# Attention scores as 64-row products in both halves of the array, V kept in float32, on one Trainium2 core

## The chip, the cores and the metric

The program runs on one core of one Trainium2 chip. The metric is the device time of one execution in microseconds; the time before is the median of three runs. A core has TensorE (PE, matrix products; its weight loads are listed as PEld), VectorE (DVE), ScalarE (ACT), GpSimd (POOL), and SyncE (SP, which here only issues DMAs). The granted clock of TensorE is given as a share of full speed: 1.00 is 2.4 GHz and 0.50 is 1.2 GHz, its two levels.

## The reference

```python
# q, k, v: (4, 8, 576, 64); M_prev (4, 8, 64, 64), z_prev (4, 8, 64), beta (8)
scores = where(causal, -1e9, (q @ k.T) / 8)
a = exp(scores - scores.max(-1)); a /= a.sum(-1) + 1e-9
local = a @ v
phi = lambda x: where(x > 0, x, exp(x) - 1) + 1
mem = (phi(q) @ M_prev) / (phi(q) @ z_prev + 1e-6)
g = 1 / (1 + exp(-beta))
x = (g * mem + (1 - g) * local)          # reshaped to 2304 rows of 512
# x is the input of a mixture of 8 experts with 1024 hidden columns, one expert for each row:
logits = normalised(x) @ normalised(expert_emb).T / tau
e = argmax(logits);  out = softmax(logits)[e] * (relu(x @ w1[e]) @ w2[e])
```

## The kernel before

Attention is done in eight groups: one of four batches and four of its eight heads. The 576 query rows of a head are cut into tiles i = 0 to 3 of 128 rows and a tail i = 4 of 64 rows, two tails of a head pair together. Causality leaves (i + 1) x 128 key columns for tile i. A score tile of 128 rows is a unit, and goes through the steps S (score products into a PSUM bank `aux`), M (VectorE adds the mask and takes the row's maximum, L725), E (ScalarE, exponential, L753), T (TensorE, transposes, L762), H and L (L772 on ScalarE and L776 on VectorE: the transposed weights as a float16 high and low part) or P (one float32 copy, L786), and C (products with V into a bank `L`).

Each group is prepared by `prep_group`: q and k are transposed on TensorE (L601), split into a high part (fp32r) and a low part, and phi(q) is formed on POOL (L667, L668: `qp`). Query and key operands are stacked by nine DMAs a group from SBUF to SBUF, so that the high parts of a head's keys stand twice, on rows 0 to 63 and 64 to 127, and the query's high and low part one above the other. A score tile is then two products for each head: one over 128 rows (L712, high and low queries with high keys) and one over 64 rows (L713, high queries with low keys). Only tiles 0 and 1 of group 0 are made directly of 64-row products (L708 to L710), since they go ahead of the first stacking.

V is prepared by `prep_v`: absolute maximum over each partition (L543, VectorE), over the partitions (`partition_all_reduce`, L547, POOL), a power of two from it (VectorE), and V scaled and split into float16 high (`vh`, L569, POOL) and low (`vl`, L572, VectorE). In tiles 0 and 3 a block of weights and V are three float16 products (L808 to L810); tiles 1, 2 and the tails use one float32 product of 65 columns (L800, L818): 64 of V and a column of ones, which gives the row's sum.

The memory term phi(q) M comes from L899; L918 to L949 put both terms together into rows X, on VectorE and POOL; `route_ops` (L983 to L1048) normalises them and forms the logits. `batch_ops` ranks rows by expert, and writes row numbers to a table in DRAM (`id_dram`) by scatters on POOL (L1128), each waiting for the one before. Three early slots of 128 rows of the first expert run ahead of the main loop of slots (L1516 layer 1, L1586 layer 2); their weights are split into high and low on ScalarE, VectorE and POOL (L1316, L1328).

The order of instructions on every engine up to the main loop is made in advance by a list scheduler (`Sched`): estimated durations (`c_act`, `c_dve` and numbers written at each `op`), priorities (`PRIO`), and rings of buffers (six PSUM banks `aux`, two `L`). Where it expects TensorE to wait near the start it inserts products that nobody reads (L255). Every engine keeps its order, so an instruction that waits holds all behind it on that engine.

Of the kernel before, what the change touches and what calls it, by code (L numbers as in the profile page):

```python
# [34 lines left out]
# Priorities and choices of the list scheduler.  # L35
PRIO = {'po': {'S': 0.5860956202798256, 'M': -2.5, 'E': 0.17467982721190245, 'T': 0.2779440791838692, 'H': -1.149000400638553, 'L': -1.05503872663039, 'C': -0.2719843589915537}, 'pa': 0.4405403455875509, 'pv': 10.001535500524492, 'sq': 2.536521872945253, 'xt': 2, 'ra': 2, 'aD': 1, 'ps': 0.775235707503454, 'lv': 2.568625074006147, 'pr': 5.21426841392578, 'rs': 1, 'w1p': 203.44655206520034, 'ag': 0, 'pb': 7.884706576128789, 'lqk': 8.346887064301836, 'rr': 0, 'aA': 1, 'pe4': 1, 'ep': 108.76714709039749, 'w2p': 229.1293559788917, 'slack': 65.79007591242566, 'pp': 1.1250262799121031, 'fc': (1, 2), 'nw2l': 2, 'nw1l': 2, 'xlo': 1, 'wpd': 2, 'w1': 300000, 'ND': 2, 'avl': 2, 'ph': 1, 'avc': 1, 'phat': 10154.340622343301, 'ae': 1}


class Sched:
    """Static list scheduler: orders single-engine steps by estimated start time, with bounded buffer rings."""  # L40
# [19 lines left out]
    def run(self, slack=80.0):  # L60
# [106 lines left out]
def kernel(  # L167
# [23 lines left out]
    ASC = 16384.0  # L191
# [32 lines left out]
    id_dram = dr.tile([PADN, 2], I32, name="id_dram")  # L224
# [4 lines left out]
    RB = cst.tile([P, 8704], F32R, name="RB")  # L229
# [5 lines left out]
    er_t = [[RA[:, 5120 + S * (2 * s + c) : 5120 + S * (2 * s + c) + S] for c in range(2)] for s in range(2)]  # L235
    loq_t = RB[:, 0:1280].rearrange("p (x n) -> p x n", x=2)
    hi_t = RB[:, 1280:3840].rearrange("p (x c n) -> p x c n", x=2, c=2)
    kh_t = [RB[:, 3840:6400].rearrange("p (x j n) -> p x j n", x=2, j=2), wk.tile([P, 2, 2, 640], F32R, tag="kh1", name="kh1")]
    lok_t = [t.rearrange("p (x n) -> p x n", x=2) for t in (RB[:, 6400:7552], RC[:, 5632:6784])]
    kl1_t = [t.rearrange("p (x n) -> p x n", x=2) for t in (RB[0:64, 7552:8704], RC[0:64, 6784:7936])]  # L240
    qs_t = [RC[:, 2816 * i : 2816 * i + 2816].rearrange("p (x j n) -> p x j n", x=2, j=2) for i in range(2)]
    qp_t = [wk.tile([P, 2, S], F32, tag=f"qp{i}", name=f"qp{i}") for i in range(2)]
    qd_t = [cst.tile([P, 2, P], F32R, name=f"qd{i}") for i in range(2)]
    VN = [wk.tile([P, NFULL + 1, 4, 65], F32, tag=f"VN{i}", name=f"VN{i}") for i in range(3)]
    VHt = [wk.tile([P, NFULL, 4, 65], F16, tag=f"vh{i}", name=f"vh{i}") for i in range(2)]
    VLt = [wk.tile([P, NFULL, 4, D], F16, tag=f"vl{i}", name=f"vl{i}") for i in range(2)]
# [19 lines left out]
    ND = cfg.get("ND", 2)  # L266

    # A unit is a 128-row score tile: the query rows of index i of some heads of one group.
    units, UB = [], []
    for gi, (b, g) in enumerate(groups):  # L270
        UB.append(float(len(units)))
        pairs = ((0, 2), (1, 3)) if gi == 0 else ((0, 1), (2, 3))
        if gi == 0 and ND > 0:
            units += [dict(gi=gi, i=0, hs=list(p)) for p in pairs]
        else:
            units.append(dict(gi=gi, i=0, hs=[0, 1, 2, 3]))
        if gi == 0 and ND < 2:
            pairs = ((0, 1), (2, 3))
        units += [dict(gi=gi, i=1, hs=list(p)) for p in pairs]
        units += [dict(gi=gi, i=i, hs=[h]) for i in (2, 3) for h in range(4)]  # L280
        units += [dict(gi=gi, i=4, x=x, hs=[2 * x, 2 * x + 1]) for x in range(2)]
    for n, u in enumerate(units):
        u["n"] = n
        u["b"], u["g"] = groups[u["gi"]]
        u["blocks"] = [(hh, kb) for hh in u["hs"] for kb in range(u["i"] + 1)] if u["i"] < 4 else range(4)
        u["direct"] = u["gi"] == 0 and u["i"] < ND
# [4 lines left out]
    # -------------------------------------------------------------- constants  # L291
    for t in qs_t:
        nc.gpsimd.memset(t[:, :, :, 0:64].bitcast(F32), 0.0)
    for t in qd_t:
        nc.gpsimd.memset(t.bitcast(F32), 0.0)
    nc.gpsimd.memset(hi_t[:, :, :, 64:128].bitcast(F32), 0.0)
    nc.gpsimd.memset(loq_t[:, :, 64:128].bitcast(F32), 0.0)
# [8 lines left out]
    for j in range(2):  # L306
# [4 lines left out]
        )  # L311
    for t in VN:
        nc.gpsimd.memset(t[:, :, :, D : D + 1], 1.0)
    for t in VHt:
        nc.gpsimd.memset(t[:, :, :, D : D + 1], 1.0)
# [36 lines left out]
    def c_pad_dma():  # L352
        nc.sync.dma_start(id_dram.rearrange("(p n) c -> p n c", p=P), padt)
# [44 lines left out]
    # -------------------------------------------------------- the experts' unit vectors  # L398
# [4 lines left out]
    def newton_steps(dst, src, s_, r_):  # L403
        """Steps of dst = sqrt(src): exponent-halving start, Newton iterations; tiny src is lifted off zero."""
# [15 lines left out]
    def chain(tag, steps, deps, prio, eng="DVE", dur=75):  # L420
# [15 lines left out]
    def en_load():  # L436
# [12 lines left out]
            # 1 / tau = tm * te with 1 <= |tm| < 2  # L449
# [27 lines left out]
    # ------------------------------------------------------------------ loads  # L477

    def load_qk(b):
        for g in range(2):  # L480
            gi, hs = 2 * b + g, slice(4 * g, 4 * g + 4)
            for s in (1, 0):
                for n in (NFULL, *range(NFULL)):
# [7 lines left out]
                    deps = () if b == 0 else tuple(("pe", gi - 2, x, s if n < NFULL else 2) for x in range(2))  # L491
# [34 lines left out]
    # ------------------------------------------------------- operand preparation  # L526
    VS = {}

    def prep_v(gi):
        b, g = groups[gi]  # L530
        st = {}
        pr = (0.0 if gi == 0 else ub(gi - 1) + cfg.get("pv", 6.0))
        lv = tuple(("lv", gi, n) for n in range(NFULL))
        vn = lambda: VN[SL["VN", gi]]
        mx, ma, scl, scw = (cst.tile([P, w], F32, name=f"v{nm}{gi % 2}") if gi < 2 else None
                            for nm, w in (("mx", 1), ("ma", 1), ("sc", 1), ("sw", 4)))
        if gi < 2:
            VS[gi] = (mx, ma, scl, scw)
        mx, ma, scl, scw = VS[gi % 2]
        dv = tuple(("d2", gi - 2, i) for i in range(5)) if gi >= 2 else ()  # L540

        def amax():
# [283 lines left out]
    def unit_ops(u):  # L826
# [6 lines left out]
        if 1 in js:  # L833
            sh += (("sh", gi, "kl", 1),)
# [1008 lines left out]
```

## Time and profile before

| | |
|---|---|
| time, median of three runs | 728.16 us (728.54, 725.67, 728.16) |
| span of the profiled execution | 719.1 us, by its trace; no time of its own beside it |
| PE, DVE, ACT, POOL busy, share of the span | 88%, 55%, 44%, 37% |
| attention, to the first early layer-1 product | 395.0 us |
| early slots, to the first main layer-1 product | 58.3 us |
| main loop of slots | 251.7 us |
| last output transfers | 14.1 us |

The median stands 9.1 us above the span: that much lies around it. The first three stages overlap a little (weights are split while attention ends), so the borders are those of TensorE's order: L1516 first runs at 395.0 us and, for the main loop, at 453.3 us.

### The profile page before, as it was taken

The page shows a single profiled execution, that of the slowest core. Times are in us where ns is not written, and L with a number is a line of the kernel's source. Part 1 is how long each engine was busy: PE and PEld are TensorE (multiplying, and loading weights), DVE is VectorE, ACT ScalarE, POOL GpSimd, SP SyncE. Part 2 cuts the span into 40 slices and gives each one's busy share as a digit, 9 for nine tenths or more (in the row PEclk, how much of TensorE's full clock was granted, in tenths as well). Part 3 has the DMA queues.
Part 4 walks back from the last instruction along what each step waited for, and adds up shares of the span by engine and source line. Part 5 has one row for each costly group of instructions (what it writes and reads, how often), then busy time and mean ns, then how long its engine had stood idle before and what let it go on. Part 6 is the DMA issues. An engine that isn't in the chain of part 4 may idle for free. (4 is left out here: it accounts for less than half of the span.)

```text
span 719.1 us, 12737 instructions
## 1 busy us (share of the span) xinstructions
PE 635.5 (88%) x3798; PEld 498.2 (69%) x3798; DVE 398.4 (55%) x1182; ACT 316.0 (44%) x646; POOL 267.9 (37%) x338
## 2 busy tenths in 40 slices
PE   7298969999998999969998876999999989988872
PEld 6267657877786787858786755777877767766651
DVE  5245535774555363734577852158535874686460
ACT  5136435764554553645467411144224541463340
POOL 6213622643735425726258343211322222231120
PEclk9658776997587585995799996999999998999996
DMA  6948860694734934405567109147734687488530
GB/s 133 213 107 185 193 145 7 156 212 84 174 87 105 203 78 105 112 7 130 99 229 161 46 6 308 40 71 195 203 91 105 207 262 201 102 228 237 161 80 13
DMA packets 153622, 98.49 MB, mean 137 GB/s; under 512 B 129080, under 2 KB 129208, under 8 KB 153538
## 3 DMA queue, kind: packets, MB, share of 16 engines
q1 hardware_dynamic: 148738, 87.02, 50.7%
q0 software_dynamic: 4800, 10.52, 4.8%
q8 instruction: 32, 0.52, 0.3%
q14 instruction: 52, 0.43, 0.2%
HBM read 110.69 MB, written 10.67 MB: 169 GB/s over the span
## 5 line engine op out<-in xcount | busy, mean ns | idle before, releaser
L1586 PE MATMUL L<-RC,hhl 128*128 128x512 f32 x528 | 140.0, 423 | 25.9 <-ACT hhl L1560 15.8
L1586 PEld LDWEIGHTS L<-RC,hhl 128*128 128x128 f32 x528 | 105.3, 203 | 53.6 <-ACT hhl L1560 17.1
L1516 PE MATMUL aux<-RB,xhl 128*128 128x512 f32 x528 | 129.8, 398 | 2.0 <-ACTq L1462 1.0
L1516 PEld LDWEIGHTS aux<-RB,xhl 128*128 128x128 f32 x528 | 98.5, 189 | 26.8 <-ACTq L1462 1.4
L725 DVE CUSTOM_DVE_ANT_0 a<-aux,mask 128x128 f32<-128x128 f32 (+3 forms) x144 | 62.6, 455 | 66.8 <-PE aux L713 59.4
L1447 POOL DMA_INDIRECT a<-x_dram,ix x22 | 23.8, 1081 | 149.6 <-DMA ix<-id_dram 111.8
L762 PE MATMUL aux<-ident,a 128*128 128x128 f32 x384 | 75.2, 333 | 3.8 <-ACT a L753 2.5
L753 ACT ACTIVATE a<-a,nb 128x128 f32<-128x128 f32 (+3 forms) x128 | 66.6, 556 | 15.2 <-DVE nb L725 10.3
L800 PE MATMUL L<-VN,aT 128*128 128x65 f32 x320 | 61.0, 351 | 6.7 <-ACT aT L786 6.4
L800 PEld LDWEIGHTS L<-VN,aT 128*128 128x128 f32 x320 | 57.3, 267 | 11.9 <-ACT aT L786 7.5
L762 PEld LDWEIGHTS aux<-ident,a 128*128 128x128 f32 x384 | 54.2, 174 | 13.4 <-ACT a L753 4.8
L786 ACT ACTIVATE aT<-aux 128x512 f32<-128x512 f32 (+1 forms) x80 | 37.0, 486 | 47.5 <-PE aux L762 46.1
L1560 ACT ACTIVATE hhl<-hT 128x1024 fp32r<-128x1024 f16 x18 | 19.0, 1058 | 69.9 <-DMA hT<-h 65.9
L943 POOL TENSOR_TENSOR A<-ms,dd 128x256 f32<-128x256 f32 (+1 forms) x40 | 25.2, 633 | 60.1 <-DVE dd L934 32.2
L1599 POOL DMA_INDIRECT out_dram<-ys,ix x22 | 25.8, 1172 | 55.7 <-DVE ys L1595 27.0
L899 PE MATMUL aux<-Mb,qp 128*128 128x130 f32 (+1 forms) x160 | 33.2, 340 | 13.0 <-POOL qp L668 13.0
L912 ACT ACTIVATE ms<-aux 128x260 f32<-128x260 f32 (+1 forms) x40 | 15.4, 386 | 53.1 <-PE aux L899 51.2
L949 POOL TENSOR_TENSOR X<-A,Xl 128x256 f32<-128x256 f32 (+1 forms) x40 | 29.3, 734 | 24.3 <-issue 20.9
L899 PEld LDWEIGHTS aux<-Mb,qp 128*128 128x128 f32 (+1 forms) x160 | 25.5, 223 | 17.1 <-POOL qp L668 13.2
L1526 ACT ACTIVATE hs<-aux 128x512 f32<-128x512 f32 x36 | 21.1, 591 | 35.4 <-PE aux L1516 35.2
L772 ACT ACTIVATE aT<-aux 128x512 f16<-128x512 f32 (+1 forms) x41 | 23.8, 584 | 27.0 <-PE aux L762 26.3
L1398 ACT ACTIVATE RC<-RA 128x1024 fp32r<-128x1024 f32 x24 | 24.7, 1054 | 21.7 <-DMA RA<-in_moe_w_dram 17.7
(280 smaller groups left out, 1224.5 us busy)
## 6 DMA issues: line engine op xcount, KB each, us to landing
RA<-in_moe_w_dram SPq DMA_DIRECT2D x172, 512.0 KB
RC<-RB SPq DMA_DIRECT2D x32, 320.0 KB
RB<-RB SPq DMA_DIRECT2D x16, 320.0 KB
kh<-RB SPq DMA_DIRECT2D x16, 320.0 KB
RA<-in_k_dram SPq DMA_DIRECT2D x32, 128.0 KB
RA<-in_q_dram SPq DMA_DIRECT2D x32, 128.0 KB
VN<-in_v_dram SPq DMA_DIRECT2D x32, 128.0 KB
x_dram<-x SPq DMA_DIRECT2D x16, 256.0 KB
```

The lines of the kernel that those rows point to most:

```text
L725: nc.vector.tensor_tensor_reduce(out=o, in0=i0, in1=i1, op0=ALU.add, op1=ALU.min, scale=-0.125, scalar=init, accum_out=acc)
L753: nc.scalar.activation(out=a[:, c], in_=a[:, c], func=AF.Exp, scale=-1.0, bias=nb[:, y : y + 1])
L762: nc.tensor.transpose(ps[:, P * y : P * y + P], a[:, P * y : P * y + P], ident)
L786: nc.scalar.activation(out=u["aT"][0:r, o : o + n], in_=t[0:r, 0:n], func=AF.Copy)
L800: nc.tensor.matmul(lt[:, 65 * hh : 65 * hh + 65], u["aT"][:, P * y : P * y + P], vn[:, kb, hh, :], start=kb == 0, stop=kb == i)
L899: nc.tensor.matmul(m[rr, 130 * x : 130 * x + 130], qp[:, x, P * i : P * i + n], Mb[b % 2][:, 2 * g + x, :], start=True, stop=True,)
L943: e.tensor_tensor(st["A"][rr], st["mv"][:, :, 0:D], i1, op=ALU.mult)
L949: e.tensor_tensor(xt, st["A"][rr], st["Xl"][rr], op=ALU.add)
L1398: nc.scalar.activation(out=h, in_=s, func=AF.Copy)
L1516: nc.tensor.matmul(G[i]["hp"][n], a[:, cc], w[:, c, 512 * n : 512 * n + 512], start=c == 0 and a is xh and w is w1h, stop=c == KD - 1 and ...
L1586: nc.tensor.matmul(G[i]["yp"], t[:, cc : cc + P], w[:, c, :], start=c == 0 and a == 0 and w is w2h, stop=c == KF - 1 and a == 1)
L1599: nc.gpsimd.indirect_dma_start(out=out[:, :], out_offset=bass.IndirectOffsetOnAxis(ap=G[i]["ix"][:, 0:1].bitcast(U32), axis=0), in_=G[i][" ...
```

## The change

A score tile is now always made of 64-row products: high x high, high x low, low x high. An even head's operands lie on rows 0 to 63, an odd head's on rows 64 to 127, and the two heads' units are issued as one step, product by product in turn, each into its own bank. Nothing is stacked any more: the 72 SBUF-to-SBUF DMAs go, `hi` and `lo` have two buffers each, and the tails' block-diagonal queries are written by ScalarE and VectorE (before: 32 copies on POOL). V stays float32: `prep_v` goes with its maximum, scale and splits, H and L become one copy P on ScalarE or VectorE, and each block of weights and V is one float32 product that streams 128 columns (65 wanted, the rest the next head's), each head at its own 128 columns of the bank. The scatters to `id_dram` carry dependencies written by hand, on the padding before them and the early loads, and none on each other. Durations, priorities and some dependencies of the scheduler are new; the rest of the order follows from them.

```diff
-    def prep_v(gi):
...
-        op(("v1", gi), "POOL", 380, lambda: nc.gpsimd.partition_all_reduce(ma, mx, P, bass.bass_isa.ReduceOp.absmax),
-           (("v0", gi),), pr)
...
+    hi_t = [t[:, 0 : 4 * S].rearrange("p (x c n) -> p x c n", x=2, c=2) for t in (RB, RC)]
+    lo_t = [t[:, 4 * S : 8 * S].rearrange("p (x c n) -> p x c n", x=2, c=2) for t in (RB, RC)]
...
-                nc.tensor.matmul(o, qs[:, x, j, c], kh[:, x, j, 128 : 128 + n], start=True, stop=False)
-                nc.tensor.matmul(o, qs[0:64, x, j, c], kl[j][0:64, x, 64 : 64 + n], start=False, stop=True)
...
+            for y in range(len(us[0]["hs"])):
+                for p, (a, c) in enumerate(((hi, hi), (hi, lo), (lo, hi))):
+                    for u in us:
+                        x, j = divmod(u["hs"][y], 2)
+                        rr = slice(64 * j, 64 * j + 64)
+                        nc.tensor.matmul(u["S"][:, y * n : y * n + n], a[rr, x, 0, P * i : P * i + P], c[rr, x, 1, 0:n],
+                                         start=p == 0, stop=p == 2)
...
-    def sH(u):
...
-    def sL(u):
...
+        lt, vn, vt = Lc[gi, i], VN[SL["VN", gi]], VNt[SL["VN", gi]]
+        if i < 4:
             for y, (hh, kb) in enumerate(u["blocks"]):
+                c = VW * kb + (D + 1) * hh
                 nc.tensor.matmul(
-                    lt[:, 65 * hh : 65 * hh + 65], u["aT"][:, P * y : P * y + P], vn[:, kb, hh, :], start=kb == 0, stop=kb == i
+                    lt[:, P * hh : P * hh + P], u["aT"][:, P * y : P * y + P], vt[:, c : c + P], start=kb == 0, stop=kb == i
                 )
...
-               d + (("crt",), ("cpadd",)) + tuple(lastsc), p0 + 1, xfer=56)
-            lastsc[:] = [("sca", bi, x)]
+            def f(x=x):
+                ins = nc.gpsimd.indirect_dma_start(
...
+                for o in id_w[:1] + id_r:
+                    tc.add_manual_dep(ins, o.name, SYNC, reason="row numbers")
...
+            op(("sca", bi, x), "POOL", 1090, f, d + (("crt",), ("cpadd",)) + tuple(lastld), p0 + 1, xfer=56)
```

The order of TensorE, in group 1, where tile 0 of four heads is made before the change: `kh1` and `RC` hold the stacked operands, `aux` is the bank.

```order
L712 MATMUL aux_1068<-kh1_81,RC_80 128x128
L713 MATMUL aux_1068<-RC_80 128x128
L712 MATMUL aux_1068<-kh1_81,RC_80 128x128
L713 MATMUL aux_1068<-RC_80 128x128
L712 MATMUL aux_1068<-kh1_81,RC_80 128x128
L713 MATMUL aux_1068<-RC_80 128x128
L712 MATMUL aux_1068<-kh1_81,RC_80 128x128
L713 MATMUL aux_1068<-RC_80 128x128
L899 MATMUL aux_1084<-Mb0_93,qp1_83 128x130 x2
```

There 128-row and 64-row products take turns, eight for four heads. After the change, also on TensorE, tile 3 of two heads of group 0 (L627 the score products, L675 transposes, L702 products with V):

```order
L579 MATMUL aux_633<-ident_68,RA_77 128x128 x4
L627 MATMUL aux_643<-RB_78 128x512
L627 MATMUL aux_644<-RB_78 128x512
L627 MATMUL aux_643<-RB_78 128x512
L627 MATMUL aux_644<-RB_78 128x512
L627 MATMUL aux_643<-RB_78 128x512
L627 MATMUL aux_644<-RB_78 128x512
L675 MATMUL aux_657<-ident_68,a_624 128x128 x4
L702 MATMUL L_578<-VN0_84,aT_652 128x128 x3
```

All six products of the step have 64 rows, and two banks take turns; full-height products stand only around the step.

On POOL, before the change, the first steps of the program after the constants are phi(q) of group 0 and the maximum and split of V:

```order
L667 TENSOR_SCALAR RA<-RA 128x576
L668 TENSOR_TENSOR qp_82<-RA 128x576
L547 ISA
L547 ISA vma_187<-vmx_186 128x1
L667 ISA
L667 TENSOR_SCALAR RA<-RA 128x576
L668 TENSOR_TENSOR qp_82<-RA 128x576
L569 TENSOR_SCALAR vh_89<-VN_86,vsc_188 128x8x64 x2
```

An `ISA` row without operands stands ahead of each reduce and ahead of the next ordinary instruction. After the change POOL's list there reads:

```order
L605 TENSOR_SCALAR RA<-RA 128x576
L606 TENSOR_TENSOR qp_82<-RA 128x576
L605 TENSOR_SCALAR RA<-RA 128x576
L606 TENSOR_TENSOR qp_82<-RA 128x576
L827 TENSOR_TENSOR A<-ms,dd 128x256
L833 TENSOR_TENSOR X<-A,Xl 128x256
```

The `ISA` rows and the splits are gone, and the assembly of X (L827, L833) follows on phi(q).

At the end of attention POOL's list before the change is this (L1328 the low part of w2, L1454 and L1447 gathers of gates and rows, L1599 the early slots' output):

```order
L949 TENSOR_TENSOR X_3394<-A,Xl 64x256
L1328 TENSOR_TENSOR RC<-RA,RC 128x1024
L1128 DMA id_dram<-idt,rpi 19456x2 x5
L1454 DMA gg<-gate_dram,ix 128x1 x3
L1447 DMA a<-x_dram,ix 128x1024 x3
L1328 TENSOR_TENSOR RC<-RA,RC 128x1024
L1599 DMA out_dram<-ys,ix 2304x512 x2
```

After the change:

```order
L1216 TENSOR_TENSOR RC<-RA,RC 128x1024 x2
L827 TENSOR_TENSOR A<-ms,dd 64x256
L833 TENSOR_TENSOR X_3057<-A,Xl 64x256
L1012 DMA id_dram<-idt,rpi 19456x2 x5
L1339 DMA a<-x_dram,ix 128x1024 x3
L1346 DMA gg<-gate_dram,ix 128x1 x3
L1490 DMA out_dram<-ys,ix 2304x512 x2
```

Both splits of w2 now stand ahead of the five scatters, and the gathers of rows ahead of those of gates.

## Rows read from the trace of the kernel before

**Rows 1.** The page's first line.

```profile
span 719.1 us, 12737 instructions
```

**Rows 2.** Windows by stage: busy PE, PEld, DVE, ACT, POOL; granted clock; DMA.

```profile
0.00:395.00 395.00, 355.81 (x2495) 278.56 (x2496) 217.68 (x799) 201.87 (x461) 185.68 (x266) 0.78 0.60 133
453.30:705.00 251.70, 233.52 (x1065) 183.53 (x1063) 149.41 (x267) 100.15 (x160) 60.90 (x54) 0.97 0.58 155
```

**Rows 3.** Waits of TensorE and ScalarE, 14 to 395 us: total, times, longest.

```profile
PE aux L899 <- POOL qp L668: 13.0, 1, 13.0
PE L L800 <- ACT aT L786: 6.4, 1, 6.4
PE L L808 <- ACT aT L772: 5.9, 1, 5.9
ACT x L983 <- POOL X L949: 20.8, 6, 8.8
```

**Rows 4.** Timeline of POOL: start, duration, instruction, idle time ahead.

```profile
21.88 0.41 POOL L547 PARTITION_ALL_REDUCE vma<-vmx  x1 [5.64 <-issue]
29.76 1.69 POOL L667 TENSOR_SCALAR RA<-RA 128x576 f32<-128x576 f32 x1 [7.47 <-issue]
...
103.83 0.68 POOL L569 TENSOR_SCALAR vh<-VN,vsc 128x512 f16<-128x512 f32 x1 [8.54 <-issue]
```

**Rows 5.** Timeline of TensorE, score products of tile 3 at full clock.

```profile
150.55 0.48 PE L712 MATMUL aux<-RB,RC 128*128 128x512 f32 x1
...
151.38 0.50 PE L712 MATMUL aux<-RB,RC 128*128 128x512 f32 x1
...
155.03 0.71 PE L721 MATMUL aux<-RB,RC 128*128 128x512 f32 x2
...
155.81 0.60 PE L762 MATMUL aux<-ident,a 128*128 128x128 f32 x4
```

**Rows 6.** The same view, 64-row products of group 0.

```profile
13.50 0.28 PE L709 MATMUL aux<-RB 64*128 64x128 f32 x2
13.61 0.29 PE L710 MATMUL aux<-RB 64*128 64x128 f32 x2
```

**Rows 7.** Score products L713 in attention, windows: PE, PEld, clock, DMA.

```profile
14.00:395.00 381.00, 61.75 (x120) 26.71 (x120) 0.77 0.59 133
```

**Rows 8.** Timeline of TensorE, products with V at full clock.

```profile
141.55 0.49 PE L762 MATMUL aux<-ident,a 128*128 128x128 f32 x3
141.88 1.67 PE L800 MATMUL L<-VN,aT 128*128 128x65 f32 x14
143.36 0.42 PE L712 MATMUL aux<-RB,RC 128*128 128x384 f32 x1
...
253.12 0.19 PE L808 MATMUL L<-vh,aT 128*128 128x65 f16 x1
...
253.21 0.19 PE L808 MATMUL L<-vh,aT 128*128 128x65 f16 x1
```

**Rows 9.** Windows of stretches at one clock level, columns as in Rows 2.

```profile
23.50:57.60 34.10, 24.62 (x94) 18.86 (x94) 12.25 (x46) 9.22 (x22) 9.39 (x13) 0.50 0.65 141
119.00:170.20 51.20, 51.05 (x471) 40.63 (x468) 36.59 (x141) 31.96 (x76) 27.30 (x36) 1.00 0.66 147
170.20:204.30 34.10, 34.04 (x141) 26.66 (x140) 17.40 (x54) 16.64 (x38) 18.85 (x22) 0.50 0.56 123
```

**Rows 10.** The second split of w2 on POOL, and TensorE's wait for it.

```profile
433.17 2.36 POOL L1328 TENSOR_TENSOR RC<-RA,RC 128x1024 fp32r<-128x1024 f32 x1
PE L L1586 <- POOL RC L1328: 8.2, 1, 8.2
```

**Rows 11.** VectorE by form, 0 to 395 us: busy us, mean ns, idle ahead.

```profile
L776 DVE SCALAR_TENSOR_TENSOR aT<-aux,aT 128x512 f16<-128x512 f32 x39 | 26.6, 685 | 11.0 <-ACT aT L772 10.7
L572 DVE SCALAR_TENSOR_TENSOR vl<-VN,vsc,vh 128x512 f16<-128x512 f32 x16 | 14.5, 904 | 24.6 <-POOL vh L569 24.5
L543 DVE TENSOR_REDUCE vmx<-VN 128x1 f32<-128x1024 f32 x8 | 9.7, 1212 | 0.1
```

More of the change, by code (lines that the diff above doesn't have):

```diff
@@ L418, in newton_steps, with chain @@
         return st
-    def chain(tag, steps, deps, prio, eng="DVE", dur=75):
+    def chain(tag, steps, deps, prio, eng="DVE", dur=155):
         for n, f in enumerate(steps):
@@ new lines, in prep_group, with pe_t @@
+        for x in range(2):
+            op(("era", gi, x), "NOP", 0, None, (("qka", gi),), pb, alloc=(("er", ("er", gi, x), 0, x),))
+        bk = ("pe", gi, 0, 2)
+        tl = lambda c: st[2][:, 0:256].rearrange("p (x c n) -> p c x n", x=2, c=2)[:, c]
+        def pe_t(bk=bk):
+            st[2] = bank(bk)
+            for x in range(2):
+                p2 = 2 * (2 * g + x)
+                for s in range(2):
+                    nc.tensor.transpose(
+                        st[2][:, 128 * x + 64 * s : 128 * x + 64 * s + 64],
+                        QK[s][NFULL][0:TAIL, p2 : p2 + 2, :].rearrange("p h d -> p (h d)"),
+                        ident[0:TAIL, 0:TAIL],
+                    )
@@ new lines, in hi_qt, with lo_qt @@
+        def hi_qt():
+            for j in range(2):
+                rr = slice(64 * j, 64 * j + 64)
+                nc.scalar.activation(out=qd[rr, 0, :, rr], in_=tl(0)[rr], func=AF.Copy)
+        def lo_qt():
+            for j in range(2):
+                rr = slice(64 * j, 64 * j + 64)
+                nc.vector.tensor_tensor(qd[rr, 1, :, rr], tl(0)[rr], qd.bitcast(F32)[rr, 0, :, rr], op=ALU.subtract)
+        pr = pb + 4 * stp
+        op(bk, "PE", 4 * e_pe, pe_t, (("lqk", gi, 0, NFULL), ("lqk", gi, 1, NFULL), ("qka", gi)), pr,
+           alloc=(("aux", bk, cfg.get("rp", 1)),))
@@ L592, in prep_group @@
+        for c, fu in ((0, AF.Exp), (1, AF.Relu)):
+            op(("ex", gi, 2, c), "ACT", c_act(128),
+               lambda c=c, fu=fu: nc.scalar.activation(out=er_t[:, c, :, 512:576], in_=tl(0), func=fu),
+               (bk, ("era", gi, 0), ("era", gi, 1)), pr + 0.3, free=(bk,))
+        for n, (x, key) in enumerate([(x, key) for x in range(2) for key in (1, 0)]):
             pr = pb + stp * n
@@ L872, in unit_ops @@
+        pv = tuple(("P", n, part) for part, _ in parts) + tuple(("lv", gi, kb) for kb in range(i + 1 if i < 4 else 5))
+        if i == 3:
+            pv += (("lv", gi, 4),)
         first, last = u["hs"][0] == 0, u["hs"][-1] == 3
@@ L927, in d2 @@
                 st["dd"][rr, 4:8], in0=lv[:, :, D : D + 1].rearrange("p h o -> p (h o)"),
-                scalar=1e-9 * (ASC if i < 4 and i not in FC else 1.0),
-                in1=(VS[gi % 2][3][rr] if i < 4 and i not in FC else invo[rr, h4]),
-                op0=ALU.add, op1=ALU.mult,
+                scalar=1e-9, in1=invo[rr, h4], op0=ALU.add, op1=ALU.mult,
             )
@@ L1096, in batch_ops @@
         ]
-        d = chain(("b", bi), steps, tuple(("lrc", x) for x in keys) + (("crt2",),), p0, dur=69 + 9 * T)
+        d = chain(("b", bi), steps, tuple(("lrc", x) for x in keys) + (("crt2",),), p0, dur=150 + 9 * T)
         def rk():
@@ L1228, in early_count @@
             ],
-            d, p0 + 5.0, dur=90,
+            d, p0 + 5.0, dur=170,
         )
@@ L1320 @@
     w2l = RC[:, 4096:8192].rearrange("p (k f) -> p k f", k=KF)
-    all_rc = tuple(("S", u["n"]) for u in units if u["gi"] >= gl - 1)
+    all_rc = tuple(u["sop"] for u in units if u["gi"] >= gl - 1 and u["duo"])
     for c in range(4):
@@ L1346, in gate_ops @@
         d += tuple(("sc2", x) for x in T_OF)
-        d = chain("gn", steps, d, p0, dur=85)
+        d = chain("gn", steps, d, p0, dur=165)
         bc = lambda x: x.unsqueeze(2).to_broadcast([P, NT, NE])
@@ L1435, in load_ids @@
         ix = ring("ix", i, 6, [P, 2], I32)
-        nc.sync.dma_start(ix, id_dram[bass.ds(ereg(1 + NEARLY + i) if i < 0 else regs[i]["off"], P), :])
+        ins = nc.sync.dma_start(ix, id_dram[bass.ds(ereg(1 + NEARLY + i) if i < 0 else regs[i]["off"], P), :]).ins
+        if i < 3:
+            for o in id_w:
+                tc.add_manual_dep(ins, o.name, SYNC, reason="row numbers")
+            id_r.append(ins)
         G[i] = dict(ix=ix)
```

440 lines of the change are left out of this document (145 added, 295 removed).

## The prediction

> **What bounds the kernel now.** I read the windows by stage first. In the first 395.0 us of the span of 719.1 us [rows 1, 2] TensorE is busy for 355.8 us at a mean granted clock of 0.78; VectorE is busy for 217.7, ScalarE for 201.9, POOL for 185.7. The reader is to see two things there: attention is a TensorE stage, and much of it is at the lower level. With levels of 1.00 and 0.50, a mean of 0.78 means 0.22 / 0.50 = 44% of the stage, 174 us, at half clock. The main loop is as full on TensorE, at 0.97 [rows 2], and none of its instructions changes.
>
> Then the waits of TensorE in attention. Three are long: 13.0 us for phi(q) from POOL, and 6.4 and 5.9 us for copies on ScalarE, which in turn stood 20.8 us behind POOL's X [rows 3]. The timeline of POOL says why POOL was late: ahead of the reduce over partitions it sits for 5.64 us with nothing to wait for, and ahead of the next ordinary instruction for 7.47 or 8.54 us, though the reduce itself takes 0.41 us [rows 4]. The eight groups have one maximum of V each (the eight L543) [rows 11], so POOL loses some 13 us eight times.
>
> Last the timeline of TensorE for prices, and windows cut where the clock changes.
>
> **The change, part by part.** All sums are against the profiled execution's 719.1 us; the median of 728.16 is 9.1 us more, and I add that at the end.
>
> *Reduces gone.* The reduces are the only instructions with this idle time on both sides, and the new POOL list has none. The three waits, 13.0 + 6.4 + 5.9, are the price: **-25**. The remaining 80 us of POOL's idle time lay under TensorE work and give nothing by themselves.
>
> *Score products.* At full clock the pair L712, L713 of a head with 512 columns takes 151.38 - 150.55 = 0.83 us, while a tail's three products of 512 columns, all of 128 rows, take 155.81 - 155.03 = 0.78, 0.26 each [rows 5]. So the pair holds 0.83 - 0.52 = 0.31 us for two changes of height, 0.155 each. For 128 columns the price is 0.11 (from L762 below), between them I interpolate: p = 0.11, 0.16, 0.21, 0.26 for tiles 0 to 3. Do two halves run at once? In group 0 two 64-row products of 128 columns, one in each half, start in every 0.11 us [rows 6], which is what one product of 128 columns takes. I take that for all widths (the other end is a rival). A new step for two units is then three product times for each pair of heads, and two changes of height. Tiles 0 and 1 have four heads in a step: before 8p + 8s, after 6p + 2s, a gain of 2p + 6s: 1.15 and 1.25 us, 7 steps each. Tiles 2 and 3 have two heads: before 4p + 4s, after 3p + 2s, a gain of p + 2s: 0.52 and 0.57 us, 16 steps each. These 14 and 32 steps are the 56 + 64 = 120 pairs of the windows [rows 7]. Sum 8.1 + 8.8 + 8.3 + 9.1 = 34.3 us at full clock, and at the mean of 0.78, 44 us: **-44**. Tails keep three products each, 0.
>
> *V in float32.* 160 triples of float16 become one product each. A triple takes 253.21 - 253.12 = 0.09 us; a float32 product of 65 columns (143.36 - 141.88) / 14 = 0.106; a float32 transpose of 128 columns (141.88 - 141.55) / 3 = 0.11 [rows 8]. So 128 columns cost about what 65 do. 160 x 0.02 is 3.2 us, and the other 160 products of tiles 1 and 2 at most 0.7; at clock 0.78 **+5**.
>
> *Relief of VectorE.* L776, L572 and L543 go: 26.6 + 14.5 + 9.7 us [rows 11]. 54 copies P come, by the order, each below the 0.685 us of L776, 37 us. VectorE falls from 217.7 to about 204 us. It is hidden by TensorE, which is the busier engine, and I count 0. If TensorE got ahead of VectorE, this would be a floor; that comes below.
>
> *The 72 DMAs.* No wait of TensorE for them is among the long ones [rows 3], so 0; they can only make room. Their issue leaves SP's queue, and what stood behind them there (loads of q, k, V) can only come earlier.
>
> *Clock.* After these three terms attention lasts 395 - 25 - 44 + 5 = 331 us, or 258 us if all were at full clock (331 x 0.78). That is the unknown: 73 us hang on it. Half-clock stretches come in two kinds. From 23.5 to 57.6 us TensorE is busy for 24.6 of 34.1 us; it follows POOL's first reduce and the 13.0 us wait [rows 3, 4, 9]. From 170.2 to 204.3 us it is busy for 34.04 of 34.10 us, and no wait stands in it [rows 9]. The first kind should vanish with its waits, the second not for any reason that I can read. Half of 73 is my value, bounds 0 and all: **-36**.
>
> *New waits.* The order is new, and each unit's chain M, E, T, P, C is as long while TensorE's work in between is shorter; two units now come out of a step together, so two maxima queue on VectorE. The nearest rows are the three waits that go, 25 us; bounds 0 and 25, value a third of that: **+8**.
>
> *End of attention.* TensorE waits 8.2 us for the second split of w2 (2.36 us), which stands behind scatters and gathers on POOL [rows 10]; now both splits are first. The scatters come later by that 2.36 us, and with them the row numbers, but they no longer wait for each other. **-8**, bounds -8 and 0.
>
> Sum: -25 - 44 + 5 - 36 + 8 - 8 = -100. 719.1 - 100 + 9.1 = **628 us**, attention ending near 303 us.
>
> **One rule that speaks against it.** In the stretch from 119.0 to 170.2 us, all at full clock, TensorE is busy for 51.05 of 51.20 us while VectorE is busy for 36.59, 71% [rows 9]. So TensorE ran unhindered with VectorE at 71%, and nothing here shows it doing so at more. If that were the limit, 204 us of VectorE would hold attention to 204 / 0.715 = 285 us. This is over the 258 us of a full clock, and under my 303. The Trainium skill, "TensorEngine Tiling (Array Packing)", section Performance Considerations (PSUM Bottleneck), states that tiling the array speeds up TensorE but not the emptying of PSUM, which may become the bottleneck; by that rule the floor of 285 us would bind where the clock is granted in full, and the sum would come to 610 us instead of 583.
>
> **The rivals.**
> 1. *The clock stays near 0.78.* For it: the stretch at 170.2 us had no wait before or in it. Then the clock's term is 0 instead of -36: 664 us; with all 25 us of new waits 681. Against it: the stretch from 23.5 us begins where POOL is late.
> 2. *Nearly full clock.* For it: several low stretches follow POOL. -73 and no new waits: attention of 258 us, 583 us in all, or 610 with VectorE's floor of 285. Against it: the stretch at 170.2.
> 3. *The halves do not overlap for wide products.* Rows show it for 128 columns only. Then tiles 2 and 3 take 6p + 2s instead of 4p + 4s: a loss of 2p - 2s, 0.11 and 0.21 us, x16 each, 5 us instead of a gain of 17; 22 us at full clock, 29 at 0.78: 657 us.
> 4. *VectorE is the pace.* Two maxima of 512 columns come at once and TensorE waits at many steps, with the clock as forecast: new waits of 25 us and more instead of 8: 645 us and up.
> 5. *Slower: the clock falls.* If new waits do to the clock what the old ones seem to have done, and there are more of them, more of the stage runs at 0.50. The time is 728 again when attention lasts 331 + 72 = 403 us (-8 at the end, +8 of waits); that is 395 us of TensorE for 258 us of work, a mean clock of 0.65, or 70% of the stage at half clock in place of 44%. At 0.60 it is 258 / 0.60 = 430 us, 763 in all. Against it: the change takes away the longest waits, and the order shows TensorE's work packed as before.
>
> **How the numbers follow.** Forecast (clock gives back a part) 0.50, at 605 to 650; clock stays 0.20; nearly full 0.15; no overlap 0.05; VectorE's pace 0.05; slower 0.05. The likeliest is 628. Both ends of the clock count as much as the bounds of the other terms: the low end takes most of the nearly-full case with its floor, 590; the high end takes the clock that stays with some new waits, 680. Outside lie the slower case and the far ends, 2 in 10. A change of under 0.5% (3.6 us) could not be told from none here. All cases but the fifth are faster by more than that: 0.93, same 0.02 (a mean clock just at the border), slower 0.05.
>
> **What would show it.** POOL has no idle time of 5 to 8 us without a releaser, and TensorE no wait over 3 us ahead of the end of attention: the first term is right. Score products start two by two, and a step of 512 columns takes about 3 x 0.26 + 0.31 = 1.09 us at full clock; about 1.9 us would be rival 3. Products with V follow each other in 0.11 us. The granted clock of attention reads about 258 / 295 = 0.87; at 0.78 the waits were not what lowered it. TensorE's waits for VectorE (L725's successors) stay under some 10 us; over 25 is rival 4. The main loop still takes 251.7 us, and the wait of 8.2 us for w2 is gone. I would be wrong above all through the clock, which no row of the kernel before settles.

## The result, and the profile after

The changed kernel takes 623.61 us (median of 4 runs, 621.05 to 624.89) against 728.35 us before in the same comparison: a ratio of 0.859, 95% interval 0.853 to 0.864. The forecast was 628 us. Its profiled execution took 622.65 us with a span of 620.9 us, so that only 1.8 us lie around the span, not the 9.1 us that I had added from the kernel before [rows 1]; that trace must be of an execution faster than the three runs shown, since about 2 us lie around the span in every later run.

From the page of the changed kernel: the span, the busy times, and the granted clock in 40 slices.

```profile
span 620.9 us, 12173 instructions
PE 549.4 (88%) x3702; PEld 456.3 (73%) x3702; DVE 369.9 (60%) x1130; ACT 296.8 (48%) x592; POOL 247.7 (40%) x282
PEclk9899999989998899969979799999999899998896
```

Windows of the changed kernel by stage (attention, early slots, main loop), columns as in Rows 2.

```profile
0.00:293.30 293.30, 268.00 (x2361) 233.79 (x2361) 188.32 (x742) 181.86 (x407) 158.29 (x206) 0.95 0.44 96
293.30:354.26 60.96, 51.55 (x277) 41.87 (x278) 31.32 (x121) 14.77 (x26) 27.00 (x22) 0.86 0.42 119
354.26:606.60 252.34, 229.72 (x1065) 180.64 (x1063) 149.52 (x267) 100.14 (x160) 61.37 (x55) 0.98 0.58 157
```

Attention went from 395.0 to 293.3 us and its clock from 0.78 to 0.95; the main loop is where it was [rows 2]. The early slots, which I had 8 us shorter, take 61.0 us instead of 58.3.

Waits of TensorE in the changed kernel, first from 14 us to the end of attention, then in the early slots.

```profile
PE aux L785 <- POOL qp L606: 10.0, 1, 10.0
PE L L702 <- ACT aT L687: 8.3, 4, 7.6
PE aux L675 <- ACT a L666: 2.1, 1, 2.1
...
PE aux L1463 <- ACT hs L1459: 6.0, 1, 6.0
```

The three waits of before are gone [rows 3]; two others, of 7.6 and 10.0 us, have come. Their places, in the timelines of POOL, of ScalarE and of TensorE (start, duration, instruction, idle time ahead):

```profile
180.85 1.08 POOL L1012 DMA_INDIRECT id_dram<-idt,rpi  x1 [3.68 <-DVE rpi L1006]
187.14 0.96 POOL L1012 DMA_INDIRECT id_dram<-idt,rpi  x1 [5.20 <-DMA id_dram<-idt,rpi]
191.03 0.96 POOL L1012 DMA_INDIRECT id_dram<-idt,rpi  x1 [2.93 <-DMA id_dram<-idt,rpi]
194.89 0.96 POOL L1012 DMA_INDIRECT id_dram<-idt,rpi  x1 [2.90 <-DMA id_dram<-idt,rpi]
198.49 0.96 POOL L1012 DMA_INDIRECT id_dram<-idt,rpi  x1 [2.64 <-DMA id_dram<-idt,rpi]
199.48 1.19 POOL L827 TENSOR_TENSOR A<-ms,dd 64x256 f32<-64x256 f32 x2
200.13 0.39 ACT L798 ACTIVATE ms<-aux 128x260 f32<-128x260 f32 x1 [8.40 <-POOL A L827]
200.96 2.29 PE L702 MATMUL L<-VN,aT 128*128 128x128 f32 x9 [7.61 <-ACT aT L687]
...
261.16 0.96 POOL L1012 DMA_INDIRECT id_dram<-idt,rpi  x1 [5.81 <-DMA id_dram<-idt,rpi]
264.48 1.40 POOL L606 TENSOR_TENSOR qp<-RA 128x576 f32<-128x576 f32 x1
265.93 0.80 PE L785 MATMUL aux<-Mb,qp 128*128 128x130 f32 x2 [10.02 <-POOL qp L606]
```

This reads from the top. Each scatter after the first waits 2.6 to 5.2 us for the DMA of the one before. **The scatters still wait for each other.** The scheduler was no longer told of an order among them and packed them; from 180.85 to 199.45 us POOL does nothing else. Its next instruction, A, holds back ScalarE's copy `ms`, which holds back the copies of weights queued behind it, and TensorE waits 7.6 us. The same near 256 us, where phi(q) stands behind four scatters.

The four low-clock stretches of attention in the changed kernel, windows with the same columns:

```profile
18.60:22.00 3.40, 3.16 (x15) 3.15 (x16) 1.80 (x8) 2.33 (x5) 1.66 (x2) 0.50 0.84 189
127.90:131.30 3.40, 3.40 (x16) 2.33 (x15) 1.77 (x4) 2.19 (x5) 2.17 (x4) 0.50 0.37 86
196.10:206.30 10.20, 5.34 (x24) 4.92 (x26) 2.75 (x9) 3.59 (x9) 6.15 (x9) 0.50 0.01 2
261.00:274.60 13.60, 8.67 (x36) 6.88 (x38) 2.64 (x12) 3.43 (x9) 7.97 (x9) 0.50 0.43 139
```

They are 31 us of 293, against 177 of 395 before, and each begins during a wait of TensorE (7.6 and 10.0 us, which began at 193.3 and 255.9 us) or within 1 us of the end of one (1.2 us up to 18.1, 2.1 us up to 127.5). None stands without one.

Steps of TensorE in the changed kernel, at full clock: score products of two heads with 512 columns, and products with V; the last row is from the page (count, busy us, mean ns).

```profile
29.25 0.96 PE L627 MATMUL aux<-RB 64*128 64x512 f32 x6
30.14 0.94 PE L702 MATMUL L<-VN,aT 128*128 128x128 f32 x6
...
285.40 1.06 PE L702 MATMUL L<-VN,aT 128*128 128x128 f32 x8
286.21 1.28 PE L635 MATMUL aux<-RC,qd 128*128 128x64 f32 x6
...
L702 PE MATMUL L<-VN,aT 128*128 128x128 f32 x640 | 89.3, 286 | 8.3 <-ACT aT L687 8.3
```

The row of this kind on the page of the kernel before, for tiles 1 and 2:

```profile
L800 PE MATMUL L<-VN,aT 128*128 128x65 f32 x320 | 61.0, 351 | 6.7 <-ACT aT L786 6.4
```

The six score products take 0.89 us (forecast 1.09), where two pairs took 1.66 before [rows 5]. Eight records with V take 0.81 us, 0.10 each, as forecast. But there are 640 of them for 320 blocks: a float32 product stands in the trace as two records, and the page of before has 320 for 160 blocks. I had counted one.

### The profile page after: what moved, and what is told of

It is laid out like the page before. It is cut to its first block, busy times and chain, and to the rows that moved or that the text cites. A ratio compares the mean times of both kernels' runs of the same rounds, so it can differ in the third digit from the quotient of the medians.

```text
span 620.9 us, 12173 instructions
## 1 busy us (share of the span) xinstructions
PE 549.4 (88%) x3702; PEld 456.3 (73%) x3702; DVE 369.9 (60%) x1130; ACT 296.8 (48%) x592; POOL 247.7 (40%) x282
## 5 line engine op out<-in xcount | busy, mean ns | idle before, releaser
L702 PE MATMUL L<-VN,aT 128*128 128x128 f32 x640 | 89.3, 286 | 8.3 <-ACT aT L687 8.3
L702 PEld LDWEIGHTS L<-VN,aT 128*128 128x128 f32 x640 | 79.5, 196 | 18.6 <-ACT aT L687 9.9
L675 PE MATMUL aux<-ident,a 128*128 128x128 f32 x384 | 61.8, 286 | 4.0 <-ACT a L666 2.1
L687 ACT ACTIVATE aT<-aux 128x512 f32<-128x512 f32 (+3 forms) x74 | 37.6, 517 | 47.1 <-PE aux L675 45.4
L827 POOL TENSOR_TENSOR A<-ms,dd 128x256 f32<-128x256 f32 (+1 forms) x40 | 26.3, 658 | 67.2 <-DVE dd L818 34.5
L675 PEld LDWEIGHTS aux<-ident,a 128*128 128x128 f32 x384 | 45.6, 146 | 9.2 <-ACT a L666 4.7
L689 DVE COPY aT<-aux 128x512 f32<-128x512 f32 (+3 forms) x54 | 29.0, 541 | 20.9 <-PE aux L675 15.7
L1012 POOL DMA_INDIRECT id_dram<-idt,rpi x18 | 18.4, 1023 | 57.0 <-DMA id_dram<-idt,rpi 46.8
L785 PE MATMUL aux<-Mb,qp 128*128 128x130 f32 (+1 forms) x160 | 26.8, 291 | 10.0 <-POOL qp L606 10.0
L1453 DVE CAST hhl<-hT 128x1024 fp32r<-128x1024 f16 x18 | 12.5, 692 | 33.5 <-DMA hT<-h 32.6
L1290 DVE TENSOR_TENSOR RC<-RA,RC 128x1024 fp32r<-128x1024 f32 x24 | 28.2, 1220 | 5.2 <-ACT RC L1286 4.9
```

Of the source, the lines that this page charges most:

```text
L675: nc.tensor.transpose(ps[:, P * y : P * y + P], a[:, P * y : P * y + P], ident)
L687: nc.scalar.activation(out=u["aT"][0:r, o : o + n], in_=t[0:r, 0:n], func=AF.Copy)
L689: nc.vector.tensor_copy(u["aT"][0:r, o : o + n], t[0:r, 0:n])
L702: nc.tensor.matmul(lt[:, P * hh : P * hh + P], u["aT"][:, P * y : P * y + P], vt[:, c : c + P], start=kb == 0, stop=kb == i)
L785: nc.tensor.matmul(m[rr, 130 * x : 130 * x + 130], qp[:, x, P * i : P * i + n], Mb[b % 2][:, 2 * g + x, :], start=True, stop=True,)
L827: e.tensor_tensor(st["A"][rr], st["mv"][:, :, 0:D], i1, op=ALU.mult)
```

## Experiments

The sums of TensorE's work below are made from the trace: for each product the time from its start to the next one's start, waits left out, times the granted clock at that moment, so in microseconds at full clock.

**1. The kernel before without the reduce.**

```diff
-        op(("v1", gi), "POOL", 380, lambda: nc.gpsimd.partition_all_reduce(ma, mx, P, bass.bass_isa.ReduceOp.absmax),
+        op(("v1", gi), "POOL", 380, lambda: nc.gpsimd.tensor_copy(ma, mx),
```

> The kernel before with the reduce over partitions replaced by a copy of each partition's own maximum on POOL (the scale is then not the same on all partitions, so the output differs; the order on TensorE is the same row for row). First theory, that the reduces cost TensorE its waits of 13.0, 6.4 and 5.9 us and with them low clock: 25 us of waits go, and of the low stretches those at 23.5, 105.4, 224.9 and 320.5 us (105 us, half of it regained): about 650 to 665 us. Rival, that only the waits go and the clock stays near 0.78: about 703 us. Second rival, that the waits move elsewhere: 715 us and more.

Measured: 662 us in the profiled run, 672 to 676 in three others (median 672.3), beside 725.8 us for the kernel before. Attention in its windows, then two of its low-clock stretches:

```profile
0.00:334.40 334.40, 312.80 (x2496) 245.24 (x2496) 215.03 (x799) 201.61 (x461) 182.40 (x266) 0.89 0.71 157
...
71.50:78.30 6.80, 6.80 (x23) 4.87 (x23) 3.35 (x11) 2.78 (x7) 0.18 (x1) 0.50 0.92 205
218.20:242.10 23.90, 23.90 (x103) 18.70 (x102) 10.38 (x45) 9.54 (x22) 7.94 (x12) 0.50 0.61 133
```

With the same order on TensorE attention is 61 us shorter in the trace, which is of the fastest execution, and its clock 0.89 instead of 0.78; by the medians the whole gain is 53 us, so that the median lies above the range of 650 to 665 us. TensorE's waits after 14 us fall from 34 to 16 us only, since others come (5.9 us of them for the stacking DMAs, at L712 and L713), but its low-clock time falls from 177 to 72 us. So the first theory holds for most of the gain, and the larger part came through the clock. Low clock remains, also in stretches where TensorE was never idle (6.80 of 6.80, 23.90 of 23.90 us) and had no wait over 0.5 us in the 5 us ahead. What lowered it there is not a wait.

**2. The kernel before with V in float32.** `'fc': (0, 1, 2, 3)` in the priorities, and `prep_v(gi)` not called (a dependency on V's scale and the choice of a later buffer go with it):

```diff
-'fc': (1, 2)
+'fc': (0, 1, 2, 3)
...
-        prep_v(gi)
```

> The kernel before with all of V's preparation left out and every product with V in float32 (65 columns), scores and planner as before. If the float32 products cost what the prediction said (+5 us) and relief of VectorE is worth nothing, it stands within 10 us of the run without the reduce, 655 to 670 us. Rival, that the work taken from VectorE and POOL was itself in the way: 15 us or more below that run. Rival, that the new order has waits of its own: above 680 us.

Measured: 688.8 us, ratio 0.942 (0.932 to 0.951); above the range of the first theory. Its attention:

```profile
0.00:359.30 359.30, 341.47 (x2299) 275.74 (x2299) 174.70 (x703) 202.29 (x463) 169.95 (x242) 0.86 0.68 147
```

TensorE is busy for 341.5 us, 29 more than in run 1, while VectorE has 40 us less to do. By the sums, products with V are 95 us at full clock instead of 76. So float32 costs TensorE 19 us at full clock, not 3.2, and with scores as before VectorE's relief does not pay for it. The second rival, waits of the new order, does not explain the time above 680 us: TensorE's waits after 14 us are 13 us, in run 1 16. But 99 us are at half clock instead of 72, which is worth some 14 of the 25 us by which attention is longer.

**3. The changed kernel with the reduces put back.** A maximum on VectorE and a reduce on POOL for each group, with no reader:

```diff
...
+        op(("v0", gi), "DVE", c_dve(1024), amax, tuple(("lv", gi, n) for n in range(NFULL)), pr, free=(("VN", gi),))
+        op(("v1", gi), "POOL", 380,
+           lambda mx=mx, ma=ma: nc.gpsimd.partition_all_reduce(ma, mx, P, bass.bass_isa.ReduceOp.absmax), (("v0", gi),), pr)
```

> The changed kernel with a maximum of V and a reduce over partitions put back in every group, which nothing reads. If the reduces were what held TensorE and lowered its clock before: 25 us of waits and 20 to 40 us of lower clock, about 655 to 690 us. Rival, that the new order hides POOL's idle time, and the gain came from the shorter score products: at most 635 us.

Measured: 692.3 us, ratio 0.954 (0.949 to 0.959), 69 us more than the changed kernel and a little over the range. Its attention window, its two largest waits of TensorE, and POOL around the first reduce:

```profile
0.00:368.70 368.70, 287.05 (x2398) 247.59 (x2398) 195.56 (x752) 184.95 (x407) 164.69 (x216) 0.87 0.35 79
...
PE aux L675 <- ACT a L666: 30.7, 5, 17.0
PE aux L785 <- POOL qp L606: 29.6, 5, 11.4
...
22.29 0.41 POOL L1573 PARTITION_ALL_REDUCE ma<-mx  x1 [5.71 <-DVE aT L689]
29.87 1.69 POOL L605 TENSOR_SCALAR RA<-RA 128x576 f32<-128x576 f32 x1 [7.17 <-issue]
```

The rival falls: the new order hides nothing of this. (The edit gives VectorE its eight maxima back as well, 1.2 us each; VectorE is busy for 53% of attention.) An instruction of 0.41 us keeps POOL from other work for some 13 us each time, eight times of eight. The Trainium skill, "GPSIMD Engine Reference", section Instruction dispatch, says that the first call to a freshly loaded kernel pays about 6 us for loading code. The 5.71 us agree with it; the 7.17 us on the way back to ordinary instructions, and that both come again at every reduce, are this trace's.

**4. The two halves' products issued one head after the other.**

```diff
-                for p, (a, c) in enumerate(((hi, hi), (hi, lo), (lo, hi))):
-                    for u in us:
+                for u in us:
+                    for p, (a, c) in enumerate(((hi, hi), (hi, lo), (lo, hi))):
```

> The changed kernel with the three products of one head issued before the three of the other, instead of in turn; nothing else differs. If the two halves run at once only when they take turns: 3 product times more for each step, 7 x (6 x 0.11 + 6 x 0.16) + 16 x (3 x 0.21 + 3 x 0.26) = 34 us at full clock, about 655 to 660 us. Rival, that the two halves do not overlap for wide products anyway: under 640 us, the loss in tiles 0 and 1 alone. Rival, that products of the next head run ahead beside the last ones: under 630 us.

Measured: 619.85 us, ratio 0.854 (0.849 to 0.860): the same as the changed kernel. The step of six, in its timeline of TensorE:

```profile
27.40 0.97 PE L627 MATMUL aux<-RB 64*128 64x512 f32 x6
28.30 0.94 PE L702 MATMUL L<-VN,aT 128*128 128x128 f32 x6
```

It takes 0.90 us. In the trace's single records the six products start two by two, 0.010 us apart, and the pairs 0.34 and 0.23 us apart. The records do not name the head, but a single full-height product of 512 columns takes 0.23 to 0.24 us in run 10, and six one after the other would take 1.4 us. So each pair is one product of each head, and the halves run side by side although one head's three products are issued first: my first theory had the wrong condition, and the rival that the second head's products run ahead is right. The same rows show that they overlap at 512 columns.

**5. Scatters that are really free.** Each writes through a view of its own, which the program's dependency tracking takes as disjoint from the others:

```diff
+    id_v = dram_disjoint_views(id_dram, NT)
...
-                    out=id_dram[:, :], out_offset
+                    out=id_v[t0 + x][:, :], out_offset
```

> The changed kernel with each scatter of row numbers writing through a view of the table of its own, so that no scatter waits for the one before; the order on every engine is the same. Theory, that the scatters still wait for each other after the change (POOL stands 46.8 us behind them) and that TensorE's waits of 7.6 us near 193 us and 10.0 us near 256 us come from there: both go, and with them the low stretches at 196 and 261 us (24 us long, half regained): 623.6 - 17.6 - 12 = 594 us, and 590 to 602 with what the early slots gain or lose. Rival, that POOL is late there for other work: 612 to 624 us.

Measured: 593.8 us, ratio 0.826 (0.823 to 0.830). Its stages, POOL at the place where the 7.6 us came from, and TensorE's longest wait in the early slots:

```profile
0.00:266.90 266.90, 259.09 (x2362) 226.30 (x2362) 188.49 (x742) 181.16 (x407) 158.20 (x206) 0.99 0.48 106
266.90:326.10 59.20, 51.03 (x277) 41.07 (x278) 30.75 (x121) 14.73 (x26) 26.75 (x22) 0.88 0.47 130
...
176.72 0.96 POOL L1014 DMA_INDIRECT id_dram<-idt,rpi  x1 [0.30 <-issue]
177.98 0.95 POOL L1014 DMA_INDIRECT id_dram<-idt,rpi  x1 [0.30 <-issue]
...
PE L L1479 <- DVE ys L1488: 3.6, 1, 3.6
```

A scatter follows the other in 1.26 us, both long waits are gone, no wait of TensorE over 2 us is left in attention after 14 us, and the clock reads 0.99. This was the cause of both waits, and the low stretches after them went too. But the early slots take 59.2 us, hardly less than the 61.0 of the changed kernel: the wait of 6.0 us is gone there, and one of 3.6 us has come.

**6. Scatters that wait, with the scheduler told so.**

```diff
-            op(("sca", bi, x), "POOL", 1090, f, d + (("crt",), ("cpadd",)) + tuple(lastld), p0 + 1, xfer=56)
+            op(("sca", bi, x), "POOL", 1090, f, d + (("crt",), ("cpadd",)) + tuple(lastld) + tuple(lastsc[-1:]), p0 + 1, xfer=56)
```

> The changed kernel with scatters that wait for each other as they do in it, but with the scheduler told of that order, so that other POOL work is put between them. Theory, that what costs is POOL's queue behind packed scatters and not the chain itself: most of the two waits go, 598 to 610 us. Rival, that the chain itself delays the table and the slots: 615 us or more.

Measured: 590.6 us, ratio 0.818 (0.814 to 0.823): lower than expected, and no slower than free scatters. Its stages:

```profile
0.00:275.30 275.30, 261.64 (x2409) 227.63 (x2409) 196.34 (x757) 183.15 (x405) 159.68 (x209) 0.99 0.47 103
275.30:327.60 52.30, 46.67 (x238) 36.69 (x238) 29.29 (x114) 9.97 (x21) 22.43 (x18) 0.90 0.28 68
```

So the chain itself costs nothing that shows; what cost was an order made without knowing of it. Both stages end at the same place, 326 and 328 us.

**7. 65 columns streamed with V instead of 128.** `lt[:, P * hh : P * hh + D + 1]` and `vt[:, c : c + D + 1]`.

> The changed kernel with 65 columns streamed in each product with V instead of 128. If a float32 product of 65 columns takes what one of 128 takes (0.106 and 0.11 us in the rows of before): within 2 us of the changed kernel. Rival, that columns count: 480 products at up to 0.05 us, about 24 us less, 600 us.

Measured: 619.7 us, ratio 0.860 (0.855 to 0.865) beside 0.859 of the changed kernel: no difference. By the sums its products with V take 72 us at full clock instead of 76; so 65 and 128 columns cost nearly the same here, as the forecast had it.

**8. Free scatters and the planned order together.** Both edits of runs 5 and 6.

> The changed kernel with free scatters as in the fifth run and the scheduler's order of the sixth (which put other POOL work between the scatters). If the two help at different places (the fifth ends attention 8 us sooner, the sixth's early slots are 7 us shorter): 578 to 588 us. Rival, that both undo the same wait and either is enough: 588 to 595 us.

Measured: 587.9 us, ratio 0.818 (0.813 to 0.822). The median lies at the border of the two expectations, but the ratio is that of run 6: the rival holds, either edit is enough. Runs 6 and 8 are the fastest versions found.

**9. Run 8 with V in two float16 parts in tiles 0 and 3, at a fixed scale.** H, L and the splits of V return from the kernel before, with 256 in the place of the scale from the maximum.

```diff
+                nc.gpsimd.tensor_scalar(VHt[SL[key]][:, ns, :, 0:D], VN[SL["VN", gi]][:, ns, :, 0:D], VSC, 0.0, op0=ALU.mult, op1=ALU.add)
...
+                nc.tensor.matmul(o, xh, vh[:, kb, hh, :], start=kb == 0, stop=False)
+                nc.tensor.matmul(o[:, 0:D], xh, vl[:, kb, hh, :], start=False, stop=False)
+                nc.tensor.matmul(o, xl, vh[:, kb, hh, :], start=False, stop=kb == i)
```

> The run before this one with V in two float16 parts again for tiles 0 and 3, but with a fixed scale of 256 in place of the maximum and no reduce (right for values of V below 255 alone). Theory, that the change paid for float32 V on TensorE, since a float32 product takes two records of 0.11 us and a triple 0.09 us: 160 x 0.13 = 21 us of TensorE come back, 560 to 573 us. Rival, that VectorE (41 us of work put back, some 20 of copies taken away, on 190 in 270) becomes the pace: no gain or a loss, 580 us or more.

Measured: 593.9 us, ratio 0.826 (0.821 to 0.831): no gain, a small loss. Its attention and its largest wait:

```profile
0.00:277.10 277.10, 257.06 (x2689) 217.41 (x2689) 207.96 (x790) 194.35 (x431) 174.36 (x227) 0.98 0.48 102
...
PE L L759 <- ACT aT L696: 7.7, 1, 7.7
```

By the sums products with V fall from 103 to 84 us, as the theory had it, but attention ends at 277 instead of 274 us (the 274 are of an execution of run 8 that took 595.19 us, 7 more than its median): TensorE's waits after 14 us rise from 7 to 16 us, and the scheduler itself filled nearly 8 us more of expected waits with products that nobody reads. VectorE stands at 75% (208 of 277), ScalarE at 70%. The price of float32 on TensorE is real; what it leaves off the other engines, which I had set to nothing, pays it back once the score products are short, at least in the order that the scheduler finds here. Which engine's relief does so is not shown: the largest wait is for ScalarE.

**10. Score products without a change of height, in run 1's kernel.**

```diff
-                nc.tensor.matmul(o, qs[0:64, x, j, c], kl[j][0:64, x, 64 : 64 + n], start=False, stop=True)
+                nc.tensor.matmul(o, qs[:, x, j, c], kh[:, x, j, 128 : 128 + n], start=False, stop=True)
```

> The kernel before without the reduce (first run) with the 64-row product of each pair replaced by a second 128-row product of the same operands (the low part of the keys is left out, the high part counted twice), so that TensorE changes height no more; the order is the same. If a pair held 0.31 us for two changes of height, 120 pairs lose 37 us at full clock in attention: 334 us become about 290 to 300. Rival, that the price lies in the products and not in the change of height: attention within 5 us of 334 us. Whether low clock that follows no wait goes as well is open; if the changes of height lower the clock, less than 25 us of the 72 us are left.

Measured: 640.4 us, ratio 0.889 (0.880 to 0.897). Attention, a pair of 512 columns with the start of the next, and the longest low-clock stretch with the wait of TensorE in which it begins:

```profile
0.00:309.80 309.80, 272.37 (x2496) 238.21 (x2496) 215.14 (x799) 198.86 (x465) 183.84 (x266) 0.90 0.78 170
...
150.66 0.40 PE L713 MATMUL aux<-kh,RC 128*128 128x512 f32 x1
150.89 0.40 PE L712 MATMUL aux<-kh,RC 128*128 128x512 f32 x1
151.13 0.39 PE L713 MATMUL aux<-kh,RC 128*128 128x512 f32 x1
...
194.90:212.00 17.10, 16.06 (x105) 14.03 (x106) 6.91 (x36) 6.79 (x19) 5.65 (x8) 0.50 0.60 130
195.94 0.27 PE L1045 MATMUL aux<-enT,xT 128*128 128x16 f16 x4 [2.78 <-DMA xT<-x]
```

A pair takes 0.47 us instead of 0.83 [rows 5], 0.36 less. The sum of score products falls from 100 to 66 us, 34 where 37 were expected; of it attention keeps 25 and ends above the 290 to 300 us expected, since TensorE's waits after 14 us rise from 16 to 32 us. So the changes of height cost what I had read. The clock stays (0.90, 61 us low instead of 72), which fails the test that I had set for it; but the stretches are others. Each of the nine low stretches of attention in this run begins during a wait of TensorE of 1.1 us or more, or within 1.5 us of the end of one. In run 1 three of six (at 71.5, 218.2 and 293.3 us), and in run 2 four of eight (at 71.5, 143.2, 190.9 and 231.9 us), begin with no wait over 0.5 us in the 5 us ahead. Low clock without a wait stands only in the kernels whose score products change height all the time, so this run speaks for the changes of height as its cause rather than against it.

## Why the prediction was right, and where it was not

The time came out 4 us from the forecast, and attention 10 us, but by errors of opposite sign: that it came so near is in part luck. Term by term:

- **Reduces gone, -25.** Right that the three waits went with them. Run 1 shows that they alone cost 61 us of attention in the trace, most of it through the clock (105 us less of it low) and 17 us through waits, and 53 us in the whole by the medians; run 3 that putting them back costs 69 us in the whole.
- **Score products, -44.** Right in its mechanism. By the sums they fall from 97 to 57 us at full clock, 40 where I had 34. Run 10 shows that 34 of such a gain come without any halves side by side, from no longer changing height.
- **V in float32, +5.** The step that failed in size: "160 triples of float16 become one product each", at 0.106. A float32 block is two records, so it costs 2 x 0.11 = 0.22 against 0.09 us, and 160 of them 21 us at full clock. By the sums products with V went from 75 to 100. The page showed it before: 320 records L800 for the 160 blocks of tiles 1 and 2.
- **Relief of VectorE and ScalarE, 0.** Probably too low: VectorE fell to 188 us, not 204, and in run 9, without the relief, the 19 us regained on TensorE are lost again in the order that the scheduler found.
- **The 72 DMAs, 0.** Not tested by itself. As long as the reduces were there, no long wait was for them; in run 1, without the reduces, TensorE waits 5.9 us for them, so 0 is probably too low as well.
- **Clock, -36.** The most uncertain term, and too small: 0.95 instead of 0.87. Before, 395 us at 0.78 are 308 us at full clock; after, 293.3 at 0.95 are 279. At 0.78 these would last 357 us, so the clock gave 64 us, near the bound of 73, and work and waits 38, where I had 56 (25 + 44 - 5 - 8).
- **New waits, +8.** 7.6 and 10.0 us of long ones, inside the bounds; but not from where I looked (maxima queueing on VectorE). They come from POOL, behind the scatters.
- **End of attention, -8.** Failed, first at "they no longer wait for each other". The dependencies written by hand do not take away the one that the program's tracking sets between writes of one table; POOL stands behind it for 46.8 us in all. The wait of 8.2 us for w2 is gone, but one of 6.0 us for ScalarE has come, which itself stood behind the gathers of rows, and one of 2.4 us for VectorE became 3.4. That is not all of it: in run 5, where the scatters are free, the early slots still take 59.2 us. The longest wait was counted for its whole length, as if none stood close behind it.
- **Around the span, 9.1.** 1.8 in truth; the trace of before was of a faster execution than the median.

Of the rivals, the second (nearly full clock) came nearest, with the longer products that I had not counted. Run 5 reaches it: 0.99 and 266.9 us of attention. The rule of the Trainium skill that I had weighed ("TensorEngine Tiling (Array Packing)", Performance Considerations, PSUM Bottleneck) did not bind in the changed kernel, where VectorE is busy for 64% of attention (188.3 of 293.3), nor in run 5, where TensorE is busy for 259.1 of 266.9 us with VectorE at 71% (188.5). That is the same share as in the rows of before [rows 9], so a floor just above it is not excluded: run 9, at 75%, has more waits of TensorE, but that VectorE is their cause is not shown.

What stays open is the low clock in runs 1 and 2 where TensorE was busy throughout and had no wait ahead, and with it the stretch at 170.2 us of before [rows 9]. It is not the reduces, which both runs leave out. In the changed kernel and in run 10 every low stretch of attention came with a wait, and these are the kernels without the steady changes of height. That the changes of height lower the clock is not shown by this, since run 10 also changed how long TensorE was busy and where it waited.

## What to carry to other kernels

Where two engines meet, price an instruction by the idle time around it, not by its own duration: a reduce of 0.41 us cost 13 us of POOL each time, and eight of them, by waits and clock, 50 to 70 us of the kernel's time. Count records, not source lines, before a product's price is multiplied. When a dependency is meant to go, look for it in the list of waits; a planner that believes it gone packs the steps that still wait, and to tell it the truth (run 6) gave as much as to make it true (run 5): 590.6 and 593.8 us against 623.6.

## What the runs showed that I had not expected

- Products in the two halves of the array overlap even if three of one half are issued ahead of three of the other: they start two by two, 0.010 us apart, and six of 512 columns take 0.90 us.
- A change between 128-row and 64-row products costs about 0.18 us at full clock (0.83 against 0.47 for a pair with two of them). By this price a full-height product with rows left empty would be cheaper than a 64-row one between two of 128; that was not run.
- Waits as short as 1.2 and 2.1 us were each followed by 3.4 us at half clock (from 18.6 and 127.9 us in the changed kernel). Not every such wait is: in runs 6 and 7 one of 1.2 us near 16 us was followed by none.
